# Fewer and larger transfers in a fused sparse-attention and mixture-of-experts kernel: values, weights, block sums and halo rows

## The chip, the core and the metric

The kernel runs on one core of a Trainium2 chip. The metric is the device time of one execution in microseconds (us). The median of three runs stands for the kernel; beside it there is one profiled execution, from which the views below are taken.

## What is computed

There are 4 batches, 8 heads, 768 tokens and 64 channels a head. First each head attends to a local window and to summaries of 24 blocks of 32 tokens:

```python
k_sum = k.reshape(B, H, nb, block, D).max(axis=3)     # block = 32, nb = 24
v_sum = v.reshape(B, H, nb, block, D).mean(axis=3)
scores_l = scale * np.matmul(q, k.transpose(0, 1, 3, 2))
mask_l = np.abs(pos[:, None] - pos[None, :]) < window  # window = 16
scores_s = scale * np.einsum('bhsd,bhnd->bhsn', q, k_sum) + np.log(block)
...
a = softmax(concat([where(mask_l, scores_l, -1e9), scores_s]))
attn_out = np.matmul(a, np.concatenate([v, v_sum], axis=2))
```

Its result, with the heads side by side, is the input x (4 x 768 x 512) of four experts, of which every token uses the best two:

```python
logits = x @ w_gate
for e in range(E):
    q, k, v = x @ wq[e], x @ wk[e], x @ wv[e]
    ye = causal_softmax(scale * q @ k.T) @ v @ wo[e]
    out += gate[:, :, e] * ye            # zero unless e is among the best two
```

All inputs and the output are float32 in device memory.

## The kernel before

The work is cut into *steps* with short names, and every step is bound to one engine. A name ends in batch b, and a pair of heads c (0 to 3) or a group g of four heads (0 or 1), sometimes with a part. The order in which the steps are issued is written out by hand in one string, TABLE; each engine (P for TensorE, V for VectorE, A for ScalarE, G for GpSimd, S for SyncE) carries out its own steps in that order, one after the other. The buffers a step uses are named in the same table, and waits between engines follow from the data and the buffers.

For each batch the first stage does the attention of the four pairs:

- `dk`, `dq` load keys and queries of four heads. They are issued on GpSimd, which converts to half precision on the way. `tk`, `tq` transpose them on TensorE; `kw`, `cq` copy the result to `kw` and `qT`; `rk` takes the block maxima.
- `dv` loads the values of a pair on SyncE into a tile `vb`, 128 partitions by 25 columns of 64 channels. A column holds what 64 queries need: partitions 32 to 95 take 64 tokens, partitions 0 to 31 take the last 32 tokens of the column before (the *halo*), and 96 to 119 the 24 block sums. The halo is not loaded: a step `hc` copies partitions 64 to 95 of each column to partitions 0 to 31 of the next.
- The block sums come in one of two ways. For batch 0 and the first half of batch 1, `bs` sums with matmuls on TensorE, `be` evicts and `ds` spreads the sums into `vb`. For the five groups in `TREE` (batch 1, second group; both groups of batches 2 and 3), `dvs` loads the values once more into a tile `vt`, where a partition holds one block of 32 tokens (8 KB), and `tr..0`, `tr..1` add the halves of a row repeatedly on GpSimd; `ds` spreads the result. There is only one buffer `vt`. It is cleared once (`vtz`), because the four loads of a group fill 24 of every 32 partitions.
- `sc`, `ex`, `av` are scores, exponential, and the product with `vb`; `rc`, `xm` normalise; `tx`, `hi`, `lo` transpose x and split it into two half-precision parts.

The second stage does the experts: `vp` (values and gate logits), `ga`, `gx`, `gb`, `gc` (gate), `pp`, `pc` (queries and keys of two experts at a time), `sp`, `es` (scores and exponential), `dm` (the causal mask on diagonal blocks, GpSimd), `aw` (product with values), `r2`, `wv`, `tw`, `ct`, `op`, `oc` and the store `od`. The weights are loaded in float32 during batch 0 into the space of two `a2` buffers (`dw` for queries and keys, `dwv`, `dwo`) and cast into place by `cw0`, `cw1`, `cvg`, `co`. Stages of neighbouring batches are interleaved in the table.

In the profile L276 issues `dk` and `dq`; L296 to L304 issue `dv`; L322 is `bs`; L357 issues `dvs` and L365 adds; L390 and L416 are `tk` and `tq`; L436 and L442 are `sc`; L459 is `av`; L517 and L523 issue the weights; L636, L660, L684 and L738 are `pp`, `sp`, `aw` and `op`; L673 is `dm`. L167 and L169 are the helper through which all copies go.

Of the kernel before, what the change touches and what calls it, by code (L numbers as in the profile page):

```python
# [24 lines left out]
PE0 = 2  # L25
TREE = {(1, 1), (2, 0), (2, 1), (3, 0), (3, 1)}
# [26 lines left out]
104,S, 2,G,0 0,G, 3,G,0 6,V, 724,A, 725,A, 726,A, 4,G, 53,P,0.0.0 55,V, 723,V, 36,P,1.1.1 37,A, 56,A, 1,G, 40,P,2.0 38,V, 41,A, 7,G,  # L53
39,V, 54,A, 57,P,1.1 58,A, 5,V, 8,G, 44,P,2.0 45,A, 10,G, 42,P,4.1 9,V, 14,S,0 16,P,0.0 727,V, 728,V, 17,V, 18,V, 24,G,1
87,P,1.2.2 70,P,0.1.0 72,V, 43,A, 61,P,2.2 71,A, 59,P,4.3 60,A, 89,V, 88,V, 13,G, 25,G,1 74,P,0.2 75,A,
91,P,6.0 92,A, 15,G, 47,P,4.0.0 19,S,1 21,P,0.1 12,G, 46,P, 22,V, 26,S,2 62,A, 73,A, 28,P,1.0 203,G,2
78,P,2.4 76,P,6.5 48,V, 49,V, 23,A, 20,G, 63,P,4.1.1 29,V, 90,G, 79,A, 27,V, 64,P, 65,V, 66,V, 77,A,
95,P,0.0 96,A, 241,P,2.0.1 242,A, 224,P,3.1.0 243,V, 11,G, 50,P,6.0.0 51,A, 31,S,3 226,V, 93,P,0.1 94,A,
67,P,4.1.1 33,P,2.1 52,V, 204,G,2 228,P,0.1 214,G,0 111,S,0 112,S, 213,G,0 68,A, 244,A, 34,V, 30,G, 35,V,
115,S, 81,P,6.0.2 69,V, 227,G, 80,P, 82,V, 229,A, 245,P,2.2 225,A, 83,V, 32,G, 246,A, 97,P,0.1.0 98,P,  # L60
114,S, 99,V, 100,V, 232,P,4.3 247,P,2.2 84,P,6.2.2 233,A, 248,A, 85,V, 86,V, 249,P,4.4 119,G, 101,P,0.3.3
258,P,2.2.2 250,A, 102,A, 103,V, 275,P,3.0.0 277,V, 121,G, 262,P,4.0 279,P,5.2 259,A, 276,A, 280,A, 260,V,
278,V, 263,A, 207,S,4 205,S,5 206,G, 165,P,0.0 167,P,6.1 261,G, 230,P,2.5 231,A, 166,V, 209,P,0.0 281,P,2.1
113,S,1 264,P,4.0 110,S, 168,V, 107,S, 116,S, 118,V, 126,P,6.0.0 282,A, 210,V, 212,A, 106,S, 109,S, 211,V,
265,A, 128,V, 127,A, 123,P,0 124,V, 129,P,2 131,A, 105,S, 108,S, 120,V, 219,S,0 125,V, 208,G, 175,P,4.0
130,V, 132,V,0 172,P,6 173,A, 373,G,1 181,P,0 182,A, 220,G, 235,P,2.0.1 234,P, 236,V, 237,V, 252,P,6.1.2
176,A, 251,P, 253,V, 254,V, 133,A, 134,V, 221,G,0 177,G, 184,P,0 266,P,2.3 185,A, 186,G, 183,G, 238,P,4.4.4
239,V, 240,V, 215,S,0 117,S, 267,A, 169,P,0 170,A, 178,P,6 179,A, 136,P,2.2 137,A, 255,P,0.5.5 256,V, 257,V,
174,G, 180,G, 135,V, 138,P,6.0 171,G, 188,P,0.0.2 189,P, 216,A, 217,S,1 187,P, 190,V, 191,V, 283,P,0.5
218,V, 139,A, 155,P,4.0 222,G, 269,P,6.0.0 378,S,0 284,A, 156,A, 143,P,0 144,A, 149,P,4 150,A, 372,G,1  # L70
146,P,2 268,P, 270,V, 271,V, 147,A, 223,G, 285,P,0.1.1 286,P, 152,P,4 140,P,6 153,A, 383,G,2 272,P,2.6.6
287,V, 288,V, 141,A, 273,V, 274,V, 289,P,0.7.7 379,G, 290,A, 291,V, 192,P,4.0 122,A, 148,G, 398,P,5.1 193,A,
399,V, 380,G,1 394,P,6.1.1 157,G, 151,G, 396,V, 415,P,7.0 416,A, 336,P,2.1 337,A, 395,V, 334,P,0.0 145,G,
142,G, 159,P,1.1.4 158,P, 154,G, 160,P, 161,V, 162,V, 376,S,2 335,A, 353,P,0.1 338,P,2 382,V, 295,P,6.1.1
297,V, 296,V, 339,A, 354,A, 397,A, 341,P,4 381,G,3 377,G, 342,A, 350,P,2 351,A, 292,P,0 293,V, 294,V,
298,P,6 299,A, 347,P,0 348,A, 400,P,2.4 374,S, 355,G, 344,P,4 300,V, 411,P,6.2.0 548,S,0 301,V,1 413,V,
345,A, 401,A, 428,P,7.0.2 430,V, 387,S,5 305,P,0.2 306,A, 163,P,4.1 164,A, 307,P,2.0 308,A, 402,P,0.2 403,A,
414,V, 429,V, 302,A, 197,P,4.0 412,V, 543,G,2 309,P,2.0 324,P,6 325,A, 553,G,0 419,P,0.3 375,G, 384,G,0
343,G, 352,G, 417,P,6.0 198,V, 303,V, 304,V, 346,G, 310,A, 349,G, 418,A, 340,G, 357,P,0.0.4 420,A, 358,P,
356,P, 359,V, 360,V, 200,P,2.1 201,A, 432,P,6.2 433,V, 321,P,0 322,A, 542,G,1 312,P,4 313,A, 361,P,7.2  # L80
549,G, 550,G,0 362,V, 194,P,2.2 552,G,4 318,P,0 319,A, 445,P,6.1.1 326,G, 195,V, 447,V, 448,V, 315,P,4
431,G, 449,P,7.1 450,V, 422,P,2.0.2 316,A, 564,P,0.2.0 566,V, 421,P, 423,V, 424,V, 405,P,4.1.0 446,A,
453,P,6.1 388,G, 404,P, 406,V, 407,V, 565,A, 454,A, 567,V, 434,P,0.5 435,A, 389,S,0 451,P,2.3 452,A, 314,G,
568,P,6.0 585,P,7.1 581,P,0.1.2 582,A, 569,A, 202,S, 323,G, 554,G,1 586,V, 317,G, 320,G, 311,G, 583,V,
327,P,1.1.4 328,P, 329,P, 330,V, 331,V, 436,P,2.0 408,P,0.0.0 437,A, 390,G, 391,G,1 393,V, 385,S,0 570,P,6.2
571,A, 584,A, 392,G, 572,P,2.4 573,A, 409,V, 425,P,4.1.1 410,V, 386,G, 196,S, 455,P,6.1.1 456,P, 426,A,
587,P,2.3 439,P,0.0.2 457,V, 458,V, 588,A, 427,V, 438,P, 602,P,2.2 440,V, 441,V, 589,P,6.1 603,A, 332,P,3.3
459,P,4.2.2 460,V, 442,P,0.3.3 461,V, 333,A, 366,P,2.1 590,A, 443,A, 444,V, 559,S,0 560,G, 561,G,1 363,P,6.2
364,A, 504,P,4.1 506,P,0.0 505,V, 367,A, 199,S, 562,V,1 465,P,2.0.0 466,V, 507,A, 523,P,0.1 517,P,4 551,G,2
524,A, 525,G, 544,S, 467,V, 518,A, 519,G, 462,P,6 463,A, 464,V, 508,P,0 511,P,2 509,A, 619,P,4.0 620,V,  # L90
615,P,5.0.1 512,A, 617,V, 468,P,6 513,G, 520,P,0 470,A, 469,V, 514,P,2 618,G, 521,A, 598,P,4.2.0 515,A,
522,G, 616,V, 369,P,6.0 370,A, 600,V, 475,P,0.2 476,A, 599,V, 555,S, 471,V,0 477,P,2.0 478,V, 545,G,
575,P,4.1.0 472,A, 510,G, 574,P, 473,V, 474,V, 368,S, 494,P,0.0 495,A, 546,S, 601,G, 604,P,2.0 623,P,6.5
576,V, 577,V, 516,G, 526,P,0.0.0 365,S, 528,P, 605,A, 527,P, 624,A, 529,V, 530,V, 621,P,2.4 622,A, 488,P,6
489,A, 547,G, 592,P,4.0.1 371,S, 496,G, 591,P, 593,V, 594,V, 606,P,0.2 607,A, 482,P,2 578,P,6.4.4 579,V,
485,P,4 483,A, 563,G,3 580,V, 486,A, 556,G, 609,P,0.1.2 608,P, 557,S, 558,G, 610,V, 611,V, 595,P,2.5.5
596,A, 479,P,4 625,P,6.0.0 480,A, 626,P, 597,V, 491,P,0 627,V, 490,G, 484,G, 628,V, 492,A, 612,P,2.6.6
613,A, 614,V, 531,P,4.0 532,V, 629,P,6.7.7 487,G, 481,G, 493,G, 499,P,1.1.0 498,P, 497,P, 500,V, 501,V,
630,A, 645,P,2.1 646,A, 647,P,4.0 648,A, 631,V, 502,P,0.1 678,P,2.2 679,V, 658,P,4.1 655,P,6 503,A,
533,P,0.1 534,V, 635,P,2.1.1 637,V, 659,A, 656,A, 661,P,4 662,A, 664,P,6 636,A, 638,P,0 639,V, 665,A,  # L100
652,P,4 653,A, 663,G, 654,G, 649,P,2 650,A, 640,A, 680,P,6.0 535,S, 681,V, 632,P,4 633,V, 657,G, 666,G,
641,V,1 697,P,0.0 698,A, 660,G, 651,G, 685,P,2 686,A, 687,G, 634,V, 536,P,6.2 537,V, 538,S, 682,P,0 699,G,
668,P,0.0.4 642,A, 683,A, 667,P, 691,P,2 692,A, 669,P, 643,V, 644,V, 674,V, 675,V, 684,G, 693,G, 670,V,
688,P,0 694,P,6 671,V, 539,P,2.0 689,A, 690,G, 701,P,1.1.0 700,P, 703,V, 704,V, 695,A, 696,G, 672,P,4.2
540,A, 541,S, 702,P, 707,V, 708,V, 673,A, 676,P,2 677,A, 705,P,3.3 709,P,2 710,V, 717,P,2.1 706,V, 718,A,
719,S, 711,P,0.2 712,V, 713,S, 714,P,4.0 715,A, 720,P,0.1 716,S, 721,A, 722,S,
# [15 lines left out]
class Plan:  # L122
# [11 lines left out]
    def emit(self, table):  # L134
        held = set()
        for i, eng, slots in table:
            if i < 0:
                self.fill(*slots)
                continue
            st = self.steps[i]  # L140
            used = [x for x in dict.fromkeys(list(st.reads) + list(st.writes) + list(st.keep))
                    if not x.cls.startswith(".")]
            new = [x for x in used if x.slot is None]
            assert len(slots) == len(new), st.name
            for w, s in zip(new, slots):
                w.slot = s
                for k in range(w.n):
                    assert (w.cls, s + k) not in held, (st.name, w.cls, s)
                    held.add((w.cls, s + k))
            st.fn(eng)  # L150
            for x in set(st.reads) | set(st.writes) | set(st.keep):
                x.left -= 1
                if x.left == 0 and x.slot is not None:
                    for k in range(x.n):
                        held.remove((x.cls, x.slot + k))


def make_plan(nc, T, q, k, v, moe_w_gate, moe_wq, moe_wk, moe_wv, moe_wo, out):
# [63 lines left out]
    def vone(e):  # L222
        for t in T["vb"]:
            en(e).memset(t[32:64, 0, 0:64], 0.0)
# [5 lines left out]
    def vzero(e, i):  # L230
# [3 lines left out]
        else:  # L234
            en(e).memset(w, 0.0)

# [47 lines left out]
    def load_v(b, c):  # L284
# [4 lines left out]
        def rows(t0, n):  # L289
            return bass.AP(vh.tensor, vh.offset + t0 * D, [[D, n], [64 * D, 1], [1, D]])  # L290

        def dv(e):
            w = T["vb"][vb[b, c].slot]
            if first:
                for h in (64, 80):
                    nc.sync.dma_start(out=w[h:h + 16, 0:1, 0:64], in_=rows(0, 16))  # L296
            else:
# [596 lines left out]
```

## Time and profile before

| | |
|---|---|
| runs | 189.85, 190.22 and 192.68 us, median 190.22 |
| profiled execution | 191.53 us, span of its instructions 189.8 us |
| mean granted TensorE clock | 0.972 |
| busy: PE, DVE, ACT, POOL | 151.4, 138.2, 124.7, 102.4 us |
| DMA | 44269 packets, 25.47 MB, mean 134 GB/s; 33264 packets under 512 B |
| chain that ended last | PE 47%, DVE 23%, DMA 10%, issue 10%, ACT 5%, POOL 3% |

PE is TensorE, DVE is VectorE, ACT is ScalarE, POOL is GpSimd and SP is SyncE. The span runs from the first to the last instruction. The page also cuts the span into 40 slices of 4.75 us and gives for each the busy share of an engine in tenths; 9 is 90% or more. Timelines give the start of a group of instructions, its length, engine, line, operation, what is written from what, and how often; in brackets the idle time of that engine before it and what ended it.

### The profile page before, as it was taken

To read this page: it belongs to the slowest core of one execution; us is meant where nothing else is said; L and a number is where in the kernel's file an instruction comes from. 1 tells how busy PE (TensorE), PEld (TensorE's weight loads), DVE (VectorE), ACT (ScalarE), POOL (GpSimd) and SP (SyncE) were. 2 spreads that over 40 slices of the span, in tenths; PEclk is the share of its full clock that TensorE was granted. 3 is DMA by queue.
4 is the path that set the end of the run, shared out by engine and by line. 5 is a ranking of instruction groups with operands and counts; after the bars stand their busy time and mean duration, and the time that the engine had idled before them with its cause. 6 is when DMAs were issued, how large, how long until landed. Compare 5 with 4: busy or idle time off the path is not lost.

```text
span 189.8 us, 6536 instructions
## 1 busy us (share of the span) xinstructions
PE 151.4 (80%) x2796; PEld 114.8 (60%) x2796; DVE 138.2 (73%) x255; ACT 124.7 (66%) x158; POOL 102.4 (54%) x156
## 2 busy tenths in 40 slices
PE   0354699809999699997997985889999799999660
PEld 0242588609868577776755675776768588565420
DVE  2669719862798899798799992977799888448730
ACT  8643266905776778896788684647794665788640
POOL 7365309492008839998799799193168720034100
PEclk9999999966999999999999999999999999999996
DMA  4999999999301489929993993960817000031426
GB/s 44 236 230 172 223 180 183 212 171 244 74 3 12 76 172 160 172 63 163 174 177 83 225 258 107 238 125 0 247 62 200 5 0 3 0 113 61 160 96 240
DMA packets 44269, 25.47 MB, mean 134 GB/s; under 512 B 33264, under 2 KB 40432, under 8 KB 43760
## 3 DMA queue, kind: packets, MB, share of 16 engines
q1 hardware_dynamic: 36784, 18.76, 43.4%
q0 software_dynamic: 7456, 6.29, 22.6%
q8 instruction: 22, 0.36, 0.9%
q14 instruction: 7, 0.06, 0.1%
HBM read 25.04 MB, written 6.29 MB: 165 GB/s over the span
## 4 chain that ended last, share of the span: by engine, by line
PE 47%; DVE 23%; DMA 10%; issue 10%; ACT 5%; POOL 3%; POOLq 0%; DVEq 0%; ACTq 0%
PE ps L459 10%; PE ps L636 8%; DMA qn<-in_q_dram 6%; PE ps L484 5%; DMA kn<-in_k_dram 4%; PE ps L568 4%; PE ps L738 4%; PE ps L660 3%; PE ps L416 3%; DVE wav L710 2%; PE ps L390 2%; DVE cmb L705 2%; PE ps L684 2%; DVE v L169 2%; PE ps L436 2%
## 5 line engine op out<-in xcount | busy, mean ns | idle before, releaser
L668 ACT ACTIVATE a<-ps 128x1024 f16<-128x1024 f32 (+1 forms) x48 | 42.0, 916 | 11.5 <-PE ps L660 10.2
L673 POOL TENSOR_SCALAR_AFFINE_SELECT a<-a 128x256 f16<-128x256 f16 x48 | 18.7, 408 | 35.8 <-ACT a L668 24.5
L449 ACT ACTIVATE aT<-ps 120x768 f32<-120x768 f32 x32 | 25.3, 817 | 8.0 <-PE ps L442 7.3
L459 PE MATMUL ps<-vb,aT 120*64 120x65 f32 x768 | 28.4, 234 | 0.6 <-POOL vb L169 0.5
L459 PEld LDWEIGHTS ps<-vb,aT 120*64 120x64 f32 x768 | 26.3, 148 | 2.9 <-issue 1.5
L365 POOL TENSOR_TENSOR vt<-vt 120x1024 f32<-120x1024 f32 (+3 forms) x20 | 24.4, 1221 | 5.1 <-DMA vt<-in_v_dram 3.8
L169 POOL COPY vb<-vb 32x1536 f32<-32x1536 f32 x13 | 18.9, 1458 | 13.9 <-issue 7.9
L636 PE MATMUL ps<-hi,wqk 128*128 128x384 f16 x128 | 22.6, 326 | 0.4 <-DVE lo L495 0.4
L400 DVE TENSOR_REDUCE ks<-ps 128x24 f16<-128x768 f16 x16 | 14.8, 946 | 7.3 <-PE ps L390 5.5
L416 PE MATMUL ps<-id,qn 128*64 128x128 f16 x192 | 9.6, 254 | 12.3 <-DMA qn<-in_q_dram 8.9
L167 ACT COPY kw<-ps 128x1152 f16<-128x1152 f16 x10 | 11.2, 1120 | 12.0 <-DVE ks L400 8.4
L660 PE MATMUL ps<-qk,qk 64*128 64x512 f16 (+3 forms) x128 | 14.9, 307 | 4.7 <-DVE wav L710 2.9
L636 PEld LDWEIGHTS <-wqk 128*128 128x128 f16 x128 | 12.0, 98 | 8.6 <-issue 1.0
L390 PE MATMUL ps<-id,kn 96*64 96x96 f16 (+1 forms) x256 | 9.0, 225 | 9.5 <-DMA kn<-in_k_dram 9.3
L495 DVE TENSOR_TENSOR lo<-ps,hi 128x768 f16<-128x768 f32 x16 | 15.1, 955 | 1.6 <-ACT hi L167 1.1
L416 PEld LDWEIGHTS <-qn 128*64 128x64 f16 x192 | 7.6, 132 | 14.2 <-DMA qn<-in_q_dram 9.4
L167 ACT COPY qT<-ps 128x768 f16<-128x768 f16 x11 | 8.6, 804 | 11.5 <-PE ps L416 10.2
L474 DVE TENSOR_TENSOR x<-ps,rec 128x768 f32<-128x768 f32 x16 | 15.3, 958 | 0.6
L484 PE MATMUL ps<-id,x 128*128 128x128 f32 x96 | 13.7, 280 | 0.9 <-DVE ks L400 0.9
L390 PEld LDWEIGHTS <-kn 96*64 96x64 f16 (+1 forms) x256 | 7.5, 123 | 11.0 <-issue 6.3
L568 PE MATMUL ps<-wvg,hi 128*128 128x264 f16 x96 | 13.9, 275 | 0.2 <-DVE lgp L169 0.2
L738 PE MATMUL ps<-wo,wT 128*128 128x512 f16 x48 | 12.0, 380 | 0.9 <-DVE wT L169 0.5
(96 smaller groups left out, 302.8 us busy)
## 6 DMA issues: line engine op xcount, KB each, us to landing
vb<-in_v_dram SPq DMA_DIRECT2D x15, 384.0 KB, 7.4
out_dram<-ob SPq DMA_DIRECT2D x11, 512.0 KB, 3.5
vt<-in_v_dram SPq DMA_DIRECT2D x20, 192.0 KB
kn<-in_k_dram POOLq DMA_DIRECT2D x7, 384.0 KB, 7.5
qn<-in_q_dram POOLq DMA_DIRECT2D x7, 384.0 KB, 7.4
a<-in_moe_wq_dram SPq DMA_DIRECT2D x4, 128.0 KB, 3.2
a<-in_moe_wk_dram SPq DMA_DIRECT2D x4, 128.0 KB, 3.2
a<-in_moe_wv_dram SPq DMA_DIRECT2D x4, 128.0 KB
```

Of the source, the lines that this page charges most:

```text
L167: nc.scalar.copy(dst, src)
L169: en(e).tensor_copy(dst, src)
L365: en(e).tensor_tensor(y[0:120], x[0:120, 0:w], x[0:120, w:2 * w], AL.add)
L390: nc.tensor.transpose(pbank16(kp)[64 * hp:64 * hp + 64, o:o + n], src[0:n, hh + hp, 64 * s:64 * s + 64], id16w(n, c0))
L416: nc.tensor.transpose(pbank16(qp)[64 * hp:64 * hp + 64, 128 * s:128 * s + 128], src[:, hh + hp, 64 * s:64 * s + 64], id16w(128))
L449: nc.scalar.activation(T["aT"][aT.slot][0:KR], pbank(sc, 2)[0:KR, :, 0:384], AF.Exp, scale=SCALE)
L459: nc.tensor.matmul(pbank(av, 2)[o:o + 64, u, 65 * (2 * (t // 2) + hp):65 * (2 * (t // 2) + hp) + 65], a[0:KR, hp, 64 * t:64 * t + 64], T[" ...
L484: nc.tensor.transpose(pbank(xp, 2)[:, t // 3, 128 * (t % 3):128 * (t % 3) + 128], T["x32"][x32.slot][:, 128 * t:128 * t + 128], T["id32"])
L568: nc.tensor.matmul(p[:, i, 0:264], hi_(ch)[:, cols], T["wvg"][:, ch, :], start=(ch == 0), stop=False, skip_group_check=True)
L636: nc.tensor.matmul(pbank(pp, 2)[:, u, 0:384], T["wqk"][:, cc, ch, j, :], hi_(ch)[:, 384 * u:384 * u + 384], start=(ch == 0), stop=(ch == N ...
L660: nc.tensor.matmul(pbank(sp, 2)[:, ep, c0:c0 + w], T["qk"][qk[1].slot][r, 128 * tj:128 * tj + 128], T["qk"][qk[0].slot][r, n0:n0 + w], sta ...
L668: nc.scalar.activation(a2v(u), pbank(sp, 2)[:, :, 0:ln], AF.Exp, scale=SCALE / (XS * XS))
```

## The change

The diff touches what is transferred how, and the table.

- **Values.** A pair's first column, loaded by a transfer of its own before, becomes part of the main one (64 partitions by 25 columns). For the pairs in the new set `EDGE` (all of batches 2 and 3) the transfer takes 96 partitions by 24 columns, halo included, and there is no `hc` step for them.
- **Block sums.** `dvs` becomes one transfer of 128 rows of 8 KB for the four heads; for the last group, where this would read past the end, one of 96 rows and one of 24. The clearing step `vtz` stays.
- **Weights.** Twelve transfers (`dw`, `dwv`) become three (`dwq`, `dwk`, `dwv`). The staging space then has the order of the source, and the casts `cw0`, `cw1`, `cvg` rearrange; `cw0` and `cw1` are two copies each.
- **Table.** It names steps instead of numbering them. On GpSimd `dk010` and `dq010` stand right after `dq000` (before: after `sel` and after `v2o`), and `dq100`, `dk110`, `dq110` right after `dk100`, ahead of `hc01`, `ksc03` and `id32`. On SyncE the whole `dwq` and `dwk` stand ahead of `dv11` and `dv10`, where half of them stood. Every other step keeps its place on its engine.
- **Clearing.** The memset of 32 partitions in the first column, done for all six `vb` buffers in `vone`, is done for one of them, in `vz0`.

```diff
+EDGE = {(b, c) for b in (2, 3) for c in range(4)}
...
         def dv(e):
             w = T["vb"][vb[b, c].slot]
+            j0, j1 = (1 if first else 0), (24 if last else 25)
+            r0, j0 = (0, 1) if (b, c) in EDGE else (32, j0)
             if first:
                 for h in (64, 80):
-                    nc.sync.dma_start(out=w[h:h + 16, 0:1, 0:64], in_=rows(0, 16))
-            else:
-                nc.sync.dma_start(out=w[64:96, 0:1, 0:64], in_=rows(-16, 32))
-            i1 = 23 if last else 24
-            src = bass.AP(vh.tensor, vh.offset + 16 * D, [[D, 64], [64 * D, i1], [1, D]])
-            nc.sync.dma_start(out=w[32:96, 1:1 + i1, 0:64], in_=src)
+                    nc.sync.dma_start(out=w[h:h + 16, 0:1, 0:64], in_=rows(0, [[D, 16], [0, 1]]))
+            nc.sync.dma_start(out=w[r0:96, j0:j1, 0:64],
+                              in_=rows(64 * j0 - 80 + r0, [[D, 96 - r0], [64 * D, j1 - j0]]))
...
+        if (b, c) in EDGE:
+            return
         def edge(e):
...
         def load(e):
-            for j in range(4):
-                nc.sync.dma_start(out=T["vt"][t.slot][32 * j:32 * j + NSUM, :],
-                                  in_=v[b, 4 * g + j].rearrange("(n s) d -> n (s d)", s=32))
+            x, vh = T["vt"][t.slot], v[b, 4 * g]
+            full = 4 if (b, g) != (B - 1, 1) else 3
+            nc.sync.dma_start(out=x[0:32 * full, :],
+                              in_=bass.AP(vh.tensor, vh.offset, [[S * D, full], [32 * D, 32], [1, 32 * D]]))
+            if full == 3:
+                nc.sync.dma_start(out=x[96:96 + NSUM, :],
+                                  in_=bass.AP(vh.tensor, vh.offset + 3 * S * D, [[32 * D, NSUM], [1, 32 * D]]))
...
+        def dwx(name, buf, o, src, to):
+            def go(e):
+                nc.sync.dma_start(out=f32(buf)[:, o:o + 1024].rearrange("p (a d) -> p a d", d=64),
+                                  in_=src.rearrange("e (c p) d -> p (e c) d", p=128))
+            R.step(name, {"S": 0.6}, [], to, go, keep=[buf], dma=2048 * 0.0178 / 16)
+        dwx("dwq", sA, 0, moe_wq, [pw[0]])
+        dwx("dwk", sA, 1024, moe_wk, [pw[1]])
+        dwx("dwv", sB, 0, moe_wv, [pv])
...
             def cw(e, i=i):
-                s = slice(1024 * i, 1024 * i + 1024)
-                copy(e, T["wqk"].rearrange("p a c j n -> p (a c j n)")[:, s], f32(sA)[:, s])
+                for j in range(2):
+                    copy(e, T["wqk"][:, i, :, j, :].rearrange("p c (a d) -> p c a d", a=2),
+                         scr(sA, 1024 * j)[:, :, 2 * i:2 * i + 2, :])
```

## The prediction

> **What bounds the kernel now.** I read the page first, then the timelines of TensorE, GpSimd, SyncE and VectorE, then the DMA view of a few short windows. Three lines of the page's 40 slices (4.75 us each) split the run in two:
>
> ```profile
> PE   0354699809999699997997985889999799999660
> PEclk9999999966999999999999999999999999999996
> DMA  4999999999301489929993993960817000031426
> ```
>
> For the first ten slices the DMA engines are full and TensorE is not: slice 8 (38 to 43 us) is empty, and its clock falls in slices 8 and 9. From 43 us on TensorE is nine tenths busy. So the start is bound by the order in which loads arrive, the rest by matmuls, with GpSimd and VectorE close behind. The empty slice, and why, in two timelines (start, length, engine, line; in brackets the idle time before it):
>
> ```profile
> 36.36 1.06 PE L322 MATMUL ps<-vb,sel 96*32 96x128 f32 x26
> 42.52 0.85 PE L416 MATMUL ps<-id,qn 128*64 128x128 f16 x12 [5.10 <-DMA qn<-in_q_dram]
> ...
> 28.50 1.46 POOL L169 COPY vb<-vb 32x1536 f32<-32x1536 f32 x1 [7.87 <-issue]
> 30.91 1.50 POOL L276 DMA_DIRECT2D qn<-in_q_dram  x2
> ```
>
> The queries of batch 1 are issued on GpSimd only at 30.91, behind a halo copy (hc01) that waited 7.87 us for the block sums on TensorE, though its buffer was free long before. TensorE stands 5.10 us for them.
>
> The second thing to see is a loop between SyncE and GpSimd. There is one vt buffer, so each load of it (dvs) waits for the last add of the tree before, and each tree waits for its load:
>
> ```profile
> 66.09 1.52 SPq L357 DMA_DIRECT2D vt<-in_v_dram  x4
> 82.97 2.08 SPq L357 DMA_DIRECT2D vt<-in_v_dram  x4
> 102.05 1.52 SPq L357 DMA_DIRECT2D vt<-in_v_dram  x4
> 115.48 1.88 SPq L357 DMA_DIRECT2D vt<-in_v_dram  x4
> ...
> 77.24 2.36 POOL L365 TENSOR_TENSOR vt<-vt 120x1024 f32<-120x1024 f32 x1
> 96.52 5.10 POOL L365 TENSOR_TENSOR vt<-vt 120x1024 f32<-120x1024 f32 x4
> 110.03 5.03 POOL L365 TENSOR_TENSOR vt<-vt 120x1024 f32<-120x1024 f32 x4
> 122.56 5.04 POOL L365 TENSOR_TENSOR vt<-vt 120x1024 f32<-120x1024 f32 x4 [3.83 <-DMA vt<-in_v_dram]
> 127.68 0.32 POOL L365 TENSOR_TENSOR vu<-vt 120x64 f32<-120x64 f32 x1
> ...
> 133.05 1.12 DVE L169 COPY vb<-vu 24x768 f32<-24x768 f32 x2
> ```
>
> From issue to first add the four late loads had 11.15, 13.55, 7.98 and 7.08 us; only the last made GpSimd wait (3.83). The trees take, first add to last, 5.70, 5.50, 5.43 and 5.44 us, 22.1 together. The last sum is spread by VectorE at 133.05 (ds32), 5 us after its tree: that is all the slack the loop has.
>
> **The change, part by part.** The order of steps on every compute engine is the same in both kernels, but for two moves and eight halo copies left out.
>
> *Keys and queries sooner.* dk010 and dq010 go from 12.13 us to about 5; dq100, dk110 and dq110 from 30.91 to about 21, right after dk100. GpSimd's issues (0.7 to 1.1 us each) cost nothing: the first two lie under its 3.77 us wait for the pi tile, the other three under the 7.87 us wait. Without that cover they would cost 1.5 and 2.6 us. The moved loads pass v and weight loads of SyncE in the shared engines; of these the nearest need is hc02 at 32.3 us, over 10 us after its load should land. The engines stay full either way, so this mostly reorders. The gain: TensorE's tq10 then follows bs03 at once (5.10 us), and VectorE's rc02, at 46.03 after 4.72 us idle, follows lo01. Before that, rk02 (21.52) stands behind ds00, which ends at 20.38 on VectorE: 1.1 us more, and the five memsets taken out of vone (about 0.2 us each) give up to 0.8. The clock stays up as well: 48 of the L459 matmuls took 2.81 us at the low clock and 1.62 later. I take 6.5 us, with bounds 0 (the loads merely swap places) and 8.
>
> *Weights in three transfers.* Bytes and 256 B packets stay the same; nine issues of about 0.5 us go from SyncE, which is off the path. dv11 and dv10 now queue behind 0.5 MB more, 2 to 5 us at the 200 GB/s of these slices; their first use is bs10 at 55.76, so nothing. cw0 and cw1 become two copies each, some 0.1 us extra; cw1 runs on GpSimd at 41.37, 11 us ahead of its matmuls.
>
> *Halo rows by DMA in batches 2 and 3.* Eight copies of 1.46 us, 11.7 us, go from GpSimd; each v load grows from 1568 to about 2300 rows of 256 B, 1 us more of DMA at some 1000 packets per us in an idle queue. In the forecast below GpSimd waits for loads there anyway, so the copies are worth nothing until the tail, where hc30 to hc33 stand ahead of masks: I take 1 us off, bounds 0 and 3.
>
> *Block sums in one transfer.* This decides. Instead of four loads of 24 rows of 8 KB there is one of 128 rows (the last: 96 and 24). On the DRAM side its outermost count is 4 heads (3 in the last), then 32 rows. No transfer before has an outermost count under 16. What the trace has is how rows of 8 KB move:
>
> ```profile
> DMA packets 77, 0.43 MB, mean 214 GB/s; under 512 B 25, under 2 KB 25, under 8 KB 25
> q1 hardware_dynamic: 77, 0.43, 87.0%
> ...
> DMA packets 15, 0.12 MB, mean 223 GB/s; under 512 B 0, under 2 KB 0, under 8 KB 0
> q1 hardware_dynamic: 15, 0.12, 59.2%
> ...
> q1 hardware_dynamic: 115, 0.24, 102.9%
> ```
>
> These are the windows 67 to 69, 84.35 to 84.9 and (2 KB rows of the output) 133.8 to 134.4 us; the last figure is the packets' time as a share of 16 engines. First: 0.87 x 16 x 2.0 us over 52 large packets is 0.53 us a row. Second: 0.592 x 16 x 0.55 over 15 is 0.35. Third: 0.086 us for 2 KB, so 0.34 for 8 KB. In the second window, with nothing but these rows in flight and more queued, 59% of the engines worked: a 24-row load doesn't use all sixteen; twelve, a divisor of 24, would fit. If the share-out goes by the outermost count, four engines carry 32 rows each. Start and landing I estimate from the output: 512 KB take 3.5 us to landing, of which 16 packets an engine x 0.086 are 1.4, so 2.1 us. A load is then 2.1 + 32 x 0.53 = 19.1 us; at 0.35 a row 13.3; at 0.63 (the last load of before: 7.08 less 2.1, over 8 rows an engine) 22.3. Spread over sixteen engines it is 2.1 + 8 x 0.35 = 4.9. I take four engines and 0.53, the row with these packets in longest succession.
>
> [...]
>
> [...]
>
> *The sum.* The first tree ended at 66.06; 6.5 sooner is 59.6 (its own load, issued near 31, has 23 us). Four loads at 19.1 are 76.4, trees 22.1: ds32 can run at 158.1 instead of 133.05, 25 us late. All of it reaches the end: VectorE takes its work in order, lg21 and v221 stand behind ds32, and TensorE stops after two more products for the banks that these empty. Masks dm215 and after stand behind the tree on GpSimd. Less 1 us of tail: 24 us. The profiled run has a span of 189.8 and took 191.5 us, 1.3 above the median of 190.2; I add 24 to the median: **214 us**.
>
> **The rivals.** (1) *The rows spread over all engines*, 4.9 us a load. Then the loop has slack everywhere and the gain at the start survives: 6.5 plus 1, less what the wait for dq310 (2.49 us at 115.6) and VectorE eat of it: 184 us. For it: 1 MB rather than 192 KB, and 128 destination rows. Against: the 59% window. (2) *Four engines, but unhindered*, 0.35 a row: 59.6 + 53.2 + 22.1 is 134.9, 1.8 late, less 1: 191 us, no change. For it: four engines ask for only 94 GB/s. Against: 0.53 as soon as rows follow closely. (3) *Four engines, hindered by key, query and v loads on the same engines*, 0.63 a row: 22.3 us a load, 170.9, 227 us. The point between slower and not is a load of about 14 us, or 0.38 a row.
>
> **How the numbers follow.** Forecast with its surroundings (0.42 to 0.6 a row, 201 to 222 us) 0.52; (1) 0.20; (2) 0.14; (3) 0.14. A measurement here tells about 2% from no change; so faster 0.20, same 0.14, slower 0.66. To leave out no more than 2 in 10 the range must reach both (1) and most of (3): 183 to 226; the forecast's own is 201 to 222.
>
> **What would show it.** In the changed profile: GpSimd's first adds at L384 waiting for vt four times, 8 to 14 us each; 19 us between a vt issue and its add; TensorE without the empty slice 8, tq10 near 36 us; digits of TensorE falling to 3 to 6 from slice 16 on; DMA share near a quarter while vt loads. If GpSimd never waits for vt, the share-out is wrong and (1) holds. If tq10 still waits, the gain is wrong and all times rise by up to 6.5 us.

## The result, and the profile after

| kernel | runs, us | median |
|---|---|---|
| before | 189.85, 190.08, 190.22, 192.68 | 190.15 |
| changed | 223.95, 224.76, 227.95, 228.96 | 226.35 |

The change makes the kernel slower by 36 us: ratio 1.176, 95% interval 1.159 to 1.194. The profiled execution took 223.95 us, with a span of 222.2 and a mean granted clock of 0.879 (0.972 before). In what follows medians are over all runs of a chip, while a ratio leaves out runs over 1.5% above the shortest of their kernel and so can stand 1 to 2% off the quotient of two medians, most of all in the second set of kernels, where one short run of the kernel before (185.24 us) leaves only three of its 23.

Of the page after, the slices (5.55 us each), the line of the tree adds, and the rows of the DMA issues:

```profile
PE   0283986599689964989504994399509999999860
PEclk9996799969969998899955899569955999999997
DMA  5999999932938756699626932492296450011335
...
L384 POOL TENSOR_TENSOR vt<-vt 120x1024 f32<-120x1024 f32 (+3 forms) x20 | 24.0, 1200 | 42.6 <-DMA vt<-in_v_dram 41.5
...
vb<-in_v_dram SPq DMA_DIRECT2D x7, 576.0 KB, 14.2
...
kn<-in_k_dram POOLq DMA_DIRECT2D x7, 384.0 KB, 13.1
qn<-in_q_dram POOLq DMA_DIRECT2D x7, 384.0 KB, 13.1
```

The empty slice at 38 us is gone, but from slice 15 on TensorE has gaps again and again, and its clock sinks with them, to 5 tenths in slices 20, 25 and 29. GpSimd, which before the change waited once for vt, now waits 41.5 us. And a key or query load needs 13.1 us from issue to landing where the page before said 7.5 and 7.4.

The loop that the prediction was about, first SyncE's issues of vt, then the trees on GpSimd, last the step on VectorE (ds32) that spreads the last sum:

```profile
62.90 0.59 SPq L373 DMA_DIRECT2D vt<-in_v_dram  x1
90.37 0.72 SPq L373 DMA_DIRECT2D vt<-in_v_dram  x1
118.37 0.55 SPq L373 DMA_DIRECT2D vt<-in_v_dram  x1
141.82 0.81 SPq L373 DMA_DIRECT2D vt<-in_v_dram  x1
...
84.67 2.34 POOL L384 TENSOR_TENSOR vt<-vt 120x1024 f32<-120x1024 f32 x1 [7.79 <-DMA vt<-in_v_dram]
112.95 5.00 POOL L384 TENSOR_TENSOR vt<-vt 120x1024 f32<-120x1024 f32 x4 [10.24 <-DMA vt<-in_v_dram]
136.39 5.01 POOL L384 TENSOR_TENSOR vt<-vt 120x1024 f32<-120x1024 f32 x4 [8.94 <-DMA vt<-in_v_dram]
158.65 5.01 POOL L384 TENSOR_TENSOR vt<-vt 120x1024 f32<-120x1024 f32 x4 [14.48 <-DMA vt<-in_v_dram]
...
164.08 1.65 DVE L181 COPY vb<-vu 24x768 f32<-24x768 f32 x2 [8.69 <-POOL vu L384]
```

Issue to first add is 21.8, 22.6, 18.0 and 16.8 us, where the kernel before had 11.2, 13.6, 8.0 and 7.1. Each load starts as its buffer comes free and each tree as its load lands: there is no slack left in the loop.

### The profile page after: what moved, and what is told of

The parts are those of the page before. It is cut to its first block, busy times and chain, and to the rows that moved or that the text cites. A ratio compares the mean times of both kernels' runs of the same rounds, so it can differ in the third digit from the quotient of the medians.

```text
span 222.2 us, 6444 instructions
## 1 busy us (share of the span) xinstructions
PE 159.6 (72%) x2796; PEld 119.2 (54%) x2796; DVE 136.2 (61%) x251; ACT 125.4 (56%) x158; POOL 91.7 (41%) x149
## 4 chain that ended last, share of the span: by engine, by line
DMA 37%; PE 30%; POOL 13%; DVE 10%; issue 6%; ACT 2%; SPq 0%; POOLq 0%; ACTq 0%; DVEq 0%
DMA vt<-in_v_dram 35%; POOL vt L384 11%; PE ps L478 6%; PE ps L653 5%; PE ps L503 2%; PE ps L337 2%; PE ps L585 2%; PE ps L677 2%; PE ps L755 2%; PE ps L435 2%; DMA kn<-in_k_dram 2%; DVE ks L419 2%; PE ps L409 2%; DVE vb L246 2%; PE ps L701 2%
## 5 line engine op out<-in xcount | busy, mean ns | idle before, releaser
L384 POOL TENSOR_TENSOR vt<-vt 120x1024 f32<-120x1024 f32 (+3 forms) x20 | 24.0, 1200 | 42.6 <-DMA vt<-in_v_dram 41.5
L690 POOL TENSOR_SCALAR_AFFINE_SELECT a<-a 128x256 f16<-128x256 f16 x48 | 18.6, 407 | 42.8 <-ACT a L685 32.7
L478 PE MATMUL ps<-vb,aT 120*64 120x65 f32 x768 | 30.9, 244 | 7.2 <-issue 6.8
L478 PEld LDWEIGHTS ps<-vb,aT 120*64 120x64 f32 x768 | 28.5, 157 | 9.7 <-issue 8.5
L677 PE MATMUL ps<-qk,qk 64*128 64x512 f16 (+3 forms) x128 | 16.2, 330 | 11.4 <-DVE v L181 10.7
L653 PE MATMUL ps<-hi,wqk 128*128 128x384 f16 x128 | 24.0, 340 | 0.0
L435 PE MATMUL ps<-id,qn 128*64 128x128 f16 x192 | 10.2, 265 | 19.0 <-DMA qn<-in_q_dram 14.8
L435 PEld LDWEIGHTS <-qn 128*64 128x64 f16 x192 | 8.1, 138 | 20.8 <-DMA qn<-in_q_dram 15.4
L409 PE MATMUL ps<-id,kn 96*64 96x96 f16 (+1 forms) x256 | 9.8, 234 | 11.8 <-DMA kn<-in_k_dram 10.1
L179 ACT COPY kw<-ps 128x1152 f16<-128x1152 f16 x10 | 11.2, 1120 | 7.3 <-DVE ks L419 6.4
L585 PE MATMUL ps<-wvg,hi 128*128 128x264 f16 x96 | 14.8, 287 | 0.6 <-DVE lgp L181 0.6
L179 ACT COPY qT<-ps 128x768 f16<-128x768 f16 x11 | 8.6, 804 | 11.2 <-PE ps L435 11.2
L503 PE MATMUL ps<-id,x 128*128 128x128 f32 x96 | 14.3, 290 | 0.5 <-DVE ks L419 0.5
L181 DVE COPY vb<-vu 24x768 f32<-24x768 f32 x6 | 4.8, 802 | 15.8 <-POOL vu L384 15.7
L677 PEld LDWEIGHTS <-qk 64*128 64x128 f16 x128 | 5.0, 97 | 16.4 <-issue 14.2
## 6 DMA issues: line engine op xcount, KB each, us to landing
kn<-in_k_dram POOLq DMA_DIRECT2D x7, 384.0 KB, 13.1
qn<-in_q_dram POOLq DMA_DIRECT2D x7, 384.0 KB, 13.1
```

The source lines that it names most:

```text
L179: nc.scalar.copy(dst, src)
L384: en(e).tensor_tensor(y[0:120], x[0:120, 0:w], x[0:120, w:2 * w], AL.add)
L409: nc.tensor.transpose(pbank16(kp)[64 * hp:64 * hp + 64, o:o + n], src[0:n, hh + hp, 64 * s:64 * s + 64], id16w(n, c0))
L435: nc.tensor.transpose(pbank16(qp)[64 * hp:64 * hp + 64, 128 * s:128 * s + 128], src[:, hh + hp, 64 * s:64 * s + 64], id16w(128))
L478: nc.tensor.matmul(pbank(av, 2)[o:o + 64, u, 65 * (2 * (t // 2) + hp):65 * (2 * (t // 2) + hp) + 65], a[0:KR, hp, 64 * t:64 * t + 64], T[" ...
L503: nc.tensor.transpose(pbank(xp, 2)[:, t // 3, 128 * (t % 3):128 * (t % 3) + 128], T["x32"][x32.slot][:, 128 * t:128 * t + 128], T["id32"])
```

## The experiments

### Is it the merged transfer, and why?

Four kernels on one chip; there the kernel before had a median of 190.31 us (13 runs).

**Four loads again (e1_four_loads).** The changed kernel with the old block-sum loads:

```
-    nc.sync.dma_start(out=x[0:32 * full, :], in_=... [[S * D, full], [32 * D, 32], [1, 32 * D]])
+    for j in range(4):
+        nc.sync.dma_start(out=T["vt"][t.slot][32 * j:32 * j + NSUM, :], in_=v[b, 4 * g + j]...)
```

> The changed kernel with the block sums loaded as before: four transfers of 24 rows. Share-out theory (a transfer uses as many engines as its outermost count allows, so the merged one has four): the four waits of 8 to 14 us at the first adds are gone, the trees keep their 5.4 us; what is left of the change is the start, where the first tree ended 3.2 us sooner (62.87 against 66.06), and about 1 us in the tail: 186 us, 184 to 189. Rival, the earlier keys and queries or the longer v loads crowd the engines, and the block sums are only the victim: it stays above 205 us, with vt still landing 15 us or more after its issue.

Measured: 189.17 us (10 runs), just above the expected range; ratio 0.986 (0.980 to 0.991), within 2% of no change. The merged transfer is worth 37 us, and all other parts together gain 1 to 3, less than expected.

**The merged load alone (e2_one_load_only).** The kernel before with the same exchange made the other way round.

> The kernel before with one thing of the change: the block sums in one transfer of 4 x 32 rows. Share-out theory: the four late loads take what they took in the changed kernel, 21.8, 22.6, 18.0 and 16.8 us, 79.2 together; the first tree ends at 66.1 as before, so the last sum is spread at 66.1 + 79.2 + 22.1 = 167.4 instead of 133.05, and the time is 190 + 34 = 224 us, 216 to 230. Rival, crowding by the moved loads: within 3 us of 190.

Measured: 233.28 us (4 runs, 226.13 to 236.48); only medians can be compared, 1.23 times the kernel before. That is above the expected range, and 7 us more than the whole change by the medians (2 by the shortest runs). Two of its waits, on GpSimd (us in total, times, longest) and on TensorE, suggest where the rest comes from:

```profile
POOL vt L369 <- DMA vt<-in_v_dram: 45.7, 4, 16.0
...
56.62 1.50 PE L394 MATMUL ps<-id,kn 98*64 98x98 f16 x32 [10.27 <-DMA kn<-in_k_dram]
```

GpSimd waits much as in the changed kernel. But keys of batch 1 are issued here at 32.27, 0.1 us after the first merged load, and land at 56.58; its last rows end at 55.1. TensorE stands 10.27 us for them. In the changed kernel they are issued at 20.8 and have landed by 31.7, before that load begins.

**One transfer, other count (e3_contiguous_rows).** The changed kernel with one pair of numbers altered:

```
-   in_=bass.AP(vh.tensor, vh.offset, [[S * D, full], [32 * D, 32], [1, 32 * D]])
+   in_=bass.AP(vh.tensor, vh.offset, [[32 * D, 32 * full], [1, 32 * D]])
```

> The changed kernel, with one number of the merged transfer changed: the 128 rows are read one behind the other from the first head on (outermost count 128, for the last load 96), instead of 4 heads x 32 rows. Same bytes, same 8 KB packets, same partitions, still one transfer; the sums of the second to fourth head of a group are those of other rows. Share-out theory: all sixteen engines, eight rows each at 0.35 to 0.6 us and 2.1 us around them, 5 to 7 us a load, no waits at the trees: 186 us, 184 to 189. Rival, one large transfer is slow as such (a megabyte in one descriptor list, or 128 partitions at once): as the changed kernel, 220 to 230 us.

Measured: 192.69 us (4 runs, 189.26 to 194.67), above the expected range but far below the rival's. 34 us of the 37 are gone with that one number, though not a byte or packet less is moved. That a large transfer is slow as such is refuted.

**Two transfers of two heads (e4_two_loads).**

```
+   for h, n in ((0, 2), (2, 2 if (b, g) != (B - 1, 1) else 1)):
+       nc.sync.dma_start(out=x[32 * h:32 * h + 32 * n, :], in_=... [[S * D, n], [32 * D, 32], [1, 32 * D]])
```

> The changed kernel with the merged transfer cut in two, each 2 heads x 32 rows. Share-out theory: two engines for each. If both transfers get the same two, 64 rows stand behind each other on each, at 0.6 us: 38 + 2 = 40 us a load, four loads +82 us, 300 us; if they get different ones, 32 rows each as in the changed kernel, 226 us. Rival, time goes by the size of the transfer: halves of 10 us that overlap or follow each other, 200 to 226 us.

Measured: 268.79 us (4 runs), ratio 1.400 (1.382 to 1.418). Smaller transfers, and far slower. How many engines worked is read from windows in which, on the hardware queue q1, next to nothing but vt rows moved. The queue lines of three such windows: four heads in one transfer (46 to 50 us of the run with two buffers, below), two heads (80 to 88 us here), and 128 rows (63.2 to 66.6 us of the contiguous kernel); the last column is the share of 16 engines:

```profile
q1 hardware_dynamic: 38, 0.31, 25.3%
```

```profile
q1 hardware_dynamic: 31, 0.25, 10.8%
```

```profile
q1 hardware_dynamic: 239, 1.02, 75.6%
```

25.3% is 4.0 engines. 10.8% is 1.7, so the two transfers of two heads shared two engines instead of getting two each; the packets of the second load took 31 us (71.6 to 102.5), 0.48 us for each of 64 rows, not the 0.6 expected. With an outermost count of 128 three quarters of all engines are busy, start and end of the load included, and it takes 6.3 us in the median from issue to landing. So the number of engines went with the outermost count in all three: 2, 4, and at least 12.

The share-out theory fits all three windows; why the two transfers of two heads got the same two engines they do not show. Whether merging paid went by that count here: merged one way the four late loads took 19.8 us on average from issue to first add, the other way a load took 6.3 from issue to landing.

### What are the other parts worth?

Four kernels on another chip, the kernel before there 189.94 us (23 runs, 185.24 to 196.02). Medians are the better guide here; by the ratios none of the four is clearly over or under 2%. All start from the kernel before, with its many transfers for the block sums.

**Early keys and queries alone (e5_early_only).**

```
- ... dq000,G, ... ds00,V, dk010,G,1 ... v2o,G, dq010,G,1 ... bs02,P,1.0 dk100,G,2 ...
+ ... dq000,G, dk010,G,1 dq010,G,1 ... vtz,G, dk100,G,2 dq100,G,2 dk110,G,0 dq110,G,0 ...
```

> The kernel before with one thing of the change: keys and queries of the first two batches issued sooner on GpSimd. By the prediction's term (6.5 us, all of it kept): 184 us. Rival theory, part of it is taken back at once: behind the wait that goes away, the twelfth matmul of the first scores of batch 1 starts only about 1.5 us after a packet of the instruction queue has landed (2.63 us of waiting at 44.12 in the changed kernel, 3.18 with four loads), and later stages wait for other things: 187 us, 185.5 to 188.5, with tq10 near 36 us and that wait of 1 to 3 us in the trace. Third case, the loads only swap places: 190.

Measured: 185.09 us (12 runs, 183.98 to 187.39), 4.9 us under the median before; ratio 0.990 (0.983 to 0.997). That is most of the prediction's 6.5 us, and the median lies below the rival's 185.5 to 188.5. Its profiled span is 182.9 against 189.8. TensorE's clock stays up, and the waits at tq10 and at the scores that follow are small:

```profile
37.40 0.36 PE L417 MATMUL ps<-id,qn 128*64 128x128 f16 x6 [1.06 <-issue]
41.98 0.20 PE L443 MATMUL ps<-qT,kw 64*128 64x64 f16 x1 [0.64 <-issue]
...
PEclk9999999999999999999999999999999999999996
```

**Halo rows by DMA alone (e6_halo_dma_only).** The v loads as in the change, in all batches and with the first column in them, the set EDGE, no hc20 to hc33, and the clearing of one buffer only.

> The kernel before with one thing of the change: the v loads as in the change, all 96 rows in batches 2 and 3, and no halo copies there. By the prediction's term (1 us, 0 to 3): 189 us. Rival, the longer v loads of 256 B packets stand in the way of the block-sum and key loads behind them, and the copies taken from GpSimd were hidden: 190 to 192.

Measured: 191.81 us (6 runs), 1.9 over the median before; ratio 1.028 (1.016 to 1.040). By the medians it costs instead of gaining; its runs (190.65 to 194.22) lie inside the scatter of the kernel before, so alone this is weak, but the next experiment but one shows it again. Which of the edits in it costs was not tried.

**Weights alone (e7_weights_only).** dwq, dwk and dwv whole, cw0, cw1 and cvg sorting them.

> The kernel before with one thing of the change: the weights in three whole transfers and the copies that sort them on the chip. By the prediction's term (nothing, 0.1 us for the copies): 190 us. Rival theory: cw0, the copy in two strided halves that VectorE makes ahead of the copy to v2 which TensorE waits for, takes 3.5 us instead of 2.4 (57.82 in the changed kernel, 60.80 before), so TensorE waits 2.8 instead of 1.7 us there: 191.1 us.

Measured: 191.93 us (6 runs), 2.0 over the median before; ratio 1.030 (1.016 to 1.044). Its runs (191.21 to 194.78) lie inside that scatter too. VectorE's cw0 and TensorE's wait behind it, before and here:

```profile
60.80 2.40 DVE L169 CAST wqk<-a 128x1024 f16<-128x1024 f32 x1
...
63.85 0.40 PE L660 MATMUL ps<-qk,qk 64*128 64x256 f16 x4 [1.66 <-DVE v L169]
```

```profile
59.80 3.53 DVE L169 CAST wqk<-a 128x512 f16<-128x512 f32 x2
...
63.98 0.40 PE L658 MATMUL ps<-qk,qk 64*128 64x256 f16 x4 [2.79 <-DVE v L169]
```

The rival is right on this point: 1.1 us more for the copy, 1.1 more for TensorE behind it.

**Early issue and halo rows (e8_early_and_halo).** Both edits together.

> The kernel before with two things of the change: early keys and queries, and the v loads with all rows; weights and block sums stay in many transfers. If the strided copies cost 1.1 us, this beats the changed kernel with four loads (1.4% under before) by about 1 us: 186.4 us. If the parts are independent and each keeps the prediction's term: 183. If the merged weights helped the start by making room in the queue: 188 or more.

Measured: 187.35 us (12 runs), 2.3 over early issue alone (12 runs each); ratio 1.001 (0.991 to 1.011). Within the scatter the parts add up: -4.9 and +1.9 make -3.0, and -2.6 is measured; with +2.0 for the weights the sum is -1.0, and the first experiment, with all three, stood 1.1 under its kernel before.

### Why do the halo rows and the weights cost, and what does a second buffer save?

Four more, the kernel before at 190.14 us (17 runs).

**A later v load (e9_halo_v_later).** In the run before this (early issue and halo rows) TensorE stood 3.42 us in the middle of a score product. The edit takes one of two v loads away from that time:

```
- ... kw32,A, dv32,S, ga2,V,0 ... od11,S, sp205,P,0.0 ...
+ ... kw32,A, ga2,V,0 ... od11,S, dv32,S, sp205,P,0.0 ...
```

> Early keys and queries and the v loads with all rows, as in the run before, but the load of the third block of batch 3 (dv32) is issued one step later on SyncE, behind the output od11 (130 us) instead of at 112.5. In the run before TensorE stood 3.42 us inside a score product at 122.55, and a packet of the instruction queue had landed at 120.83 after waiting among rows of two v loads; with short v loads the same place cost 0.65 us, the packet having started 2.5 us sooner. Theory, v rows delay TensorE's instructions: without the second v load that wait falls below 1 us and the time by 2 to 3 us, to 185 us. Rival, the halo rows cost their 2 us elsewhere (at the trees, or by the clock): 187 us, whether the wait shrinks or not.

Measured: 186.88 us (12 runs), ratio 0.992 (0.988 to 0.997), within the scatter of 187.35. The wait is untouched:

```profile
122.67 0.40 PE L446 MATMUL ps<-qT,kw 64*128 64x64 f16 x8 [3.42 <-issue]
```

The theory as put, that the second v load delays TensorE, falls; the first still runs at that time. Where the cost stands can be read from the traces of the other runs: this wait is 0.78 us in the kernel before and 0.65 with early issue alone, but 3.43 with halo rows alone and 3.42 with both. These 2.7 us more are about what the halo rows cost. Why the product goes on later stays open: the four-load and the contiguous kernel load halo rows too and wait 1.11 and 1.90 us there.

**The same on the fastest kernel (e10_early_v_later).**

> Early keys and queries alone, as in the fastest run so far (185.1 us), with dv32 issued behind od11 as well. Theory of delayed instructions: only 0.65 us is left to win at that place: 184.5 us, 184 to 185.5. Rival, a later v load is missed by the work on batch 3: 186 or more.

Measured: 185.78 us (6 runs), ratio 0.988 (0.982 to 0.994): no gain over 185.09.

**One copy for the weights (e11_weights_one_copy).**

```
-    for j in range(2):
-        copy(e, T["wqk"][:, i, :, j, :]..., scr(sA, 1024 * j)[:, :, 2 * i:2 * i + 2, :])
+    copy(e, w.rearrange("p c j (a d) -> p j a c d", a=2), src[:, :, 2 * i:2 * i + 2, :, :])
```

> The weights in three whole transfers alone, with cw0 and cw1 as one instruction each instead of two. In the trace of the two halves each half on VectorE ends 0.3 us after an add of the tree on GpSimd has ended (1.8 us a half, 3.5 together), the one whole copy of before likewise after the first add (2.40), and a copy of the same size with strided rows takes 0.68 us where GpSimd adds nothing. Theory, the price is that two instructions each wait for an add: 2.4 us again for cw0 and 1.66 for TensorE's wait, and the time 1 us below that with halves, 190.8 us. Rival, strided rows are slow as such: 3.5 us and 192.

Measured: cw0 is back at one piece of 2.39 us and TensorE's wait at 1.65:

```profile
57.20 5.37 POOL L365 TENSOR_TENSOR vt<-vt 120x1024 f32<-120x1024 f32 x4
...
57.71 2.39 DVE L169 CAST wqk<-a 128x1024 f16<-128x1024 f32 x1
...
60.76 0.40 PE L658 MATMUL ps<-qk,qk 64*128 64x256 f16 x4 [1.65 <-DVE v L169]
```

So strided rows are not what is slow; the number of instructions that run beside the tree is: 2.39 us as one, 3.53 as two. In time it is 191.48 us (6 runs, 188.39 to 195.41), ratio 1.011 (1.001 to 1.020): 0.45 below the two halves, too little for this scatter. The second instruction explains at most 1.1 of the 2.0 us.

**Two buffers (e12_two_buffers).** The changed kernel, vt=2 in SLOTS, each dvs issued one tree sooner.

> The changed kernel with a second vt buffer: each merged load of 4 x 32 rows is issued one tree sooner. Theory, four engines with 32 rows each are busy for 18 to 20 us per load whoever waits: five loads from 36 us on end near 136, so the last tree ends at 142 and the last sum is spread some 9 us later than in the kernel before, 198 us, 194 to 206, keys and queries that land late included. Rival, the loss is only the wait of each load for the tree ahead of it: the loads hide under the other work, 187 to 190 us.

Measured: 213.72 us (4 runs), ratio 1.134 (1.123 to 1.144). Neither theory: the trees hardly wait any more, and two thirds of the loss stay. GpSimd's only wait for vt, TensorE's two longest waits, and the landing of the key loads issued between 70 and 92 us, while a vt load was under way:

```profile
140.63 5.03 POOL L372 TENSOR_TENSOR vt<-vt 120x1024 f32<-120x1024 f32 x4 [2.30 <-DMA vt<-in_v_dram]
...
89.58 0.85 PE L397 MATMUL ps<-id,kn 98*64 98x98 f16 x16 [8.37 <-DMA kn<-in_k_dram]
123.17 0.85 PE L423 MATMUL ps<-id,qn 128*64 128x128 f16 x12 [11.82 <-DMA qn<-in_q_dram]
```

```profile
kn<-in_k_dram POOLq DMA_DIRECT2D x2, 384.0 KB, 16.9
```

The keys issued at 72.71 land at 89.5, 1.0 us after the last vt row (88.5); the queries issued at 98.80 land at 117.8, 1.7 after it (116.1), and the next ones behind them. One reading would be that a share of each load waits on the four busy engines; which engines carried it was not shown. Either way, what is issued behind the merged transfer lands late here: these keys took 16.9 us in the median, against 7.5 in the kernel before. TensorE's two waits, 20.2 us together, are most of the 23.6 by which this kernel is slower than the one before.

## Why the prediction was right, and where it was not

**Direction and mechanism: right.** Four engines for an outermost count of 4 (the 25.3% above), the four waits at L384 (foreseen 8 to 14 us each, found 7.8 to 14.5), and the passing of all of it to the end, were found as written; the contiguous kernel shows the first, the four-load kernel the rest. The kernel before has no transfer with such a count: the four engines of the sum were the author's choice, with the 59% window of a 24-row load behind it. The rival of all sixteen engines is refuted, and so is that of four unhindered ones: a row's packet took 0.56 to 0.59 us in the first three loads and 0.40 in the last two, against 0.35. No run shows the 0.6 us a row at which the forecast's own range ends as a fixed price: with next to nothing else moving, the 25.3% above are 0.43 us a row (0.253 x 16 x 4.0 us over 38).

**The size: 12 us too small, and its main term right by luck.** The median, 226.35, stands at the edge of the whole range and above the forecast's own 201 to 222, next to the 227 of rival (3). In the terms of the sum (issue to first add, less 2.1 us, over 32 rows) the four late loads took 0.62, 0.64, 0.50 and 0.46 us a row: the first two as rival (3) prices loads that others hinder, the last two faster than forecast. That their mean, 0.55, comes near the assumed 0.53 is luck. By the prediction's own sum the span would have been 213.9 (last sum at 158.1, then 56.75 as before, less 1). It is 222.2, with the last sum at 164.08:

| term | predicted | trace | difference, us |
|---|---|---|---|
| end of the first tree | 59.6 | 62.9 | +3.3 |
| four loads | 76.4 | 79.2 | +2.8 |
| trees and joints | 22.1 | 22.0 | -0.1 |
| from there to the end | 55.75 | 58.1 | +2.4 |

The remaining 4 us are not in this trace: the profiled execution is the shortest of four, 2.4 below their median, and 1.3 were taken off for the execution before.

**The first tree** rests on the term *Keys and queries sooner*. The 6.5 us were there: tq10 moved from 42.52 to 35.58, rc02 on VectorE from 46.03 to 39.45, and alone the early issue keeps 4.9 to 6.9 us. In the changed kernel half was lost again before the first tree ended. Most of it is a wait of TensorE inside the first scores of batch 1; of the window from 40.9 to 42.8 us the DMA view shows, on the queue called instruction, one packet of 16 KB:

```profile
q8 instruction: 1, 0.02, 5.7%
...
44.12 0.19 PE L461 MATMUL ps<-qT,kw 64*128 64x64 f16 x1 [2.63 <-issue]
...
45.82 1.54 PE L503 MATMUL ps<-id,x 128*128 128x128 f32 x6
```

The last line is the rest, some 1.1 us: behind the wait the granted clock is lower (6 in slice 8 of the changed kernel), and these six matmuls take 1.54 us instead of 0.88 before.

5.7% of 16 engines in 1.9 us is the 1.7 us that this packet took; it landed at 42.69, and TensorE went on 1.4 us later. The same product waits 3.18 and 2.63 us in the four-load and the contiguous kernel, which load merged weights at that time, but 0.64 and 0.56 in the early-issue and the early-issue-and-halo kernel, which do not; in those with two transfers and with two buffers, where dwo is held up for 25 us behind vt, 0.31 and 0.65. The merged load alone, with twelve transfers for the weights, stands between at 1.19. With weights alone, where TensorE comes to this product some 6 us later, it doesn't wait at all. That the merged weights delay the packet fits most of these, but was only argued.

**Weights at nothing** was wrong: +2.0 alone. The step failed at "two copies each, some 0.1 us extra": it counted the instructions, not what runs beside them. cw0 takes 1.1 us more and TensorE waits 1.1 more behind it, at 62.01 in the changed kernel, just as the first tree ends; the rest of the 2.0 is not explained.

**Halo rows, 1 us gained** was wrong in sign: +1.9 alone, +2.3 on top of early issue. That the saved copies were hidden, as forecast, fits. The cost shows as 2.7 us more in one wait of TensorE (e9 above); its cause was not found.

**The missing step** is what the vt load does to others. The third rival let keys and v loads hinder the vt load; the reverse, 13.1 us to landing instead of 7.5 and TensorE standing 4.67 us for keys (86.24) and 10.86 for queries (119.46), is in no term:

```profile
86.24 0.54 PE L409 MATMUL ps<-id,kn 98*64 98x98 f16 x16 [4.67 <-DMA kn<-in_k_dram]
119.46 0.85 PE L435 MATMUL ps<-id,qn 128*64 128x128 f16 x12 [10.86 <-DMA qn<-in_q_dram]
```

That the sum came close all the same is luck again: those waits lie largely beside the waits of GpSimd, so that the one covers the other. With two buffers GpSimd's are gone, and two thirds of the loss are still there.

**A reading that was wrong** stands in rival (1): the 2.49 us at 115.6 are taken for a wait for dq310, but the row says issue, eight matmuls into its group. No run shows them as a wait for that load.

**What beats both kernels**: early keys and queries alone, 185.09 us in 12 runs against 189.94 in 23.

## What to carry to other kernels

Before several loads are merged into one, look at the outermost dimension of the merged pattern, here on the DRAM side: a count of 4 here put 1 MB on four engines (25.3% of 16), and the same megabyte with a count of 128 took a third of the time (6.3 us to landing, against 19.8 to the first add). Price such a load twice: for who waits for it, and for every transfer issued behind it, which here landed late (keys and queries after 13.1 us instead of 7.5 and 7.4); the second buffer took away only the first (GpSimd's wait 2.30 us instead of 41.5), and the kernel still took 213.72 us. And time the parts of a change one by one: here, by the medians, one part gained 5 us, two lost about 2 each, and one lost 37.

## What the runs showed that was not expected

- TensorE went on soon after packets of a DMA queue called instruction. In the changed kernel the twelfth matmul of a group of scores stood 2.63 us and went on 1.4 us after a 16 KB packet of that queue had landed (42.69); with early issue and halo rows a score product stood 3.42 us and went on 1.7 us after such a packet (120.83). That TensorE waits for what these packets bring was not shown.
- The cast cw0 on VectorE, beside tree adds on GpSimd, ended only when an add had ended. Of 128x1024, cvg takes 0.68 us where no add runs; cw0 takes 2.40 beside them, and in two halves 3.53, each time ending 0.3 to 0.6 us after an add. What makes it wait was not shown.
- Two transfers of count 2 in one queue kept two engines busy between them (10.8% of 16), not four.
- While a slow merged load was queued, SyncE itself stood at later issues: 14.28 us at 41.94 in the changed kernel, 26.02 at 39.28 in the one with two buffers.
